# Transposes and value products of a segment loop, split into TensorE's four column groups

## The chip, the cores and the metric

The kernel runs on one core of one Trainium2 chip. The metric is the device time of one execution in microseconds (us). The engines are called as in the profile: PE is TensorE's matmul, PEld its weight load, DVE is VectorE, ACT is ScalarE, POOL is GpSimd, SP is SyncE, which only issues DMAs here.

## The reference

Two independent computations are put side by side in the output. Part A is attention with a recurrent memory: 64 segments of 32 rows, in each of which 8 memory rows and the segment's rows attend to each other, and the first 8 rows of the result are the next segment's memory. So the segments depend on each other in order. Part B is a long convolution with a state-space kernel; the change doesn't touch it.

```python
for s in range(n_seg):                       # 64 segments of 32 rows
    h = concatenate([mem, xs], axis=1)       # 8 + 32 rows of 1024
    q, k, v = (einsum('btd,dhe->bhte', h, W) for W in (Wq, Wk, Wv))   # 32 heads of 128
    scores = einsum('bhqe,bhke->bhqk', q, k) * scale
    p = softmax(where(mask, scores, -1e9))
    o = einsum('bhqk,bhke->bhqe', p, v)
    o = einsum('bhte,hed->btd', o, Wo)
    mem = o[:, :8]
    outs.append(o[:, 8:])
```

## The kernel before, in words

Part B and everything of part A that doesn't depend on the memory come first (some 700 us). Among the latter are q, k and v of the last 8 rows of every segment, which are kept in memory outside the core as PKd and VXd. The loop then runs over 64 segments with a state `hT` of 32 rows (24 rows of x, 8 of the memory), held as 8 chunks of 128 x 32. After the loop a last product (L617, some 55 us) finishes the output of the rows that were computed ahead.

A matmul has a stationary operand (loaded into the array by a weight load, PEld) and a moving one that streams through. The array's 128 output columns can be used as one, or as four column groups of 32, each with a weight load and a matmul of its own: `tile_position=(0, 32*g)`, with the output in partitions 32g to 32g+31. With 32 rows in `hT`, the large products of the loop use the groups:

- **Projections** (`quads`, L371): for each of 8 chunks (a unit, 128 x 2048 of a weight), four matmuls in the four groups, `hT` stationary, 512 columns of weight moving. The products are k0, q0, k1, q1, v0 and v1 (two halves of the heads).
- **Scores** (`scores`, L396 and L400): 32 matmuls in the groups, 40 columns moving.
- **Output projection** (`oproj`, L481): four matmuls in the groups for each head, 256 columns moving.

Between them stand pieces that use all 128 columns at once:

- **`tr`** (L382): four transposes of 128 x 128 turn the evacuated k or q (`evac`, L377) so that the head dimension lies on the partitions. They stand twice in a segment, eight at a time: k0 and q0 between the groups of k1, k1 and q1 between the groups of v0.
- **`pv`** (L450, L454): values times probabilities. V is stationary, and the spread-out probabilities `pb` (four matmuls) and those of the 8 ahead-computed keys, `lbs`, move. It is called four times in a segment: `pv_x` and `pv_l` for the first half of the heads, between the groups of v1; `pv_x` for the second half, inside the output projection; and `pv_l` for the second half, after it.
- **`tro`** (L580): two transposes of the new memory, which DVE copies into `hT` (L582). The next segment starts from there.

Around them, in the order written out by hand: ACT evacuates a projection (L377), copies a mask into the score buffer (L390), copies transposed q and k (L497, L517, L518; DVE L496 has k0), takes the exponentials (L416) and evacuates the products with the values (L467: `o0`, `o1`) and the result (L574). POOL adds the ahead-computed keys to KT (`put_kl`, L385, after the load of PKd) and spreads probabilities (L443, L438). DVE does the maxima, sums and 32 x 32 transposes of the softmax and spreads probabilities (L412 to L438: `pb`, `lb1`). L435 makes `pb`, and L438 makes `lb1`.

Most of the weights stay in the core. Twelve units of 512 KB in each segment don't fit and are streamed: SP issues them in order into four slots (`wst`, tags w0 to w3), and a slot is filled again when the matmuls that read it are done. Two units more are kept in PSUM and copied out by DVE (`fetch`, L292).

Of the kernel before, what the change touches and what calls it, by code (L numbers as in the profile page):

```python
# [30 lines left out]
        ("o", 15): (("Oa", 1024, 512), ("Ob", 1536, 384), (None, 1920, 128))}  # L31
HALF = (("q", 0, 7), ("o", 15))
SLOTS = 4

ARENA = 5984
AT = {"K7a": 3072, "K7b": 1024, "K7c": 2048, "K7d": 4192, "ob": 4960, "pk": 0, "vx": 3392, "Q7a": 2048, "Q7b": 3072,
# [21 lines left out]
def streamed_keys():  # L58
    return [key for key in [(m, t, kc) for (m, t), kcs in STREAM.items() for kc in kcs] + [("o", u) for u in STREAM_O]]
# [173 lines left out]
def part_a(ctx, tc, x, src, WD, HE, seg_len, out_a, ahead, W_res, rest, places, first):  # L233
    nc = tc.nc
# [13 lines left out]
    ident, mask, BD, BDx, BDL, hT = ahead.consts  # L248
# [6 lines left out]

    loads = [SLOTS]

# [36 lines left out]
    def stage(key, in_):  # L294
        t_ = wst.tile([128, 2048], BF16, name="wst", tag="w%d" % (loads[0] % SLOTS))
        loads[0] += 1
        nc.sync.dma_start(out=t_[:].rearrange("e (h d) -> e h d", h=2) if len(in_.shape) == 3 else t_[:], in_=in_)
        return t_

    def load_kept(key):  # L300
# [3 lines left out]
        if key in HALF:  # L304
            w = wst.tile([128, 2048], BF16, name="wst", tag="w%d" % (loads[0] % SLOTS))
            loads[0] += 1
# [56 lines left out]
    for s in range(NS):  # L363
        def quads(m, t, kcs, a=None):
            if a is None:
                a = ps.tile([128, 512], F32, name="acc", tag=BANK[m, t])
            for kc in kcs:
                w = unit((m, t, kc))
                for g in range(4):
                    for o_, rhs in columns(w, 512 * g, 512):  # L370
                        nc.tensor.matmul(a[32 * g:32 * g + 32, o_:o_ + rhs.shape[1]], lhsT=hT[:, kc, :], rhs=rhs,  # L371
                                         start=(kc == 0), stop=(kc == KC - 1), tile_position=(0, 32 * g), skip_group_check=True)
            return a
# [5 lines left out]

        def tr(q, p):  # L380
            for hl in range(4):
                nc.tensor.transpose(out=p[:, hl, :, :].rearrange("p a b -> p (a b)"), in_=q[:, 128 * hl:128 * hl + 128], identity=ident[:])  # L382

        def put_kl(KT, t):
            nc.gpsimd.tensor_copy(out=KT[:, :, :, SL:NK], in_=kl[t])  # L385
# [61 lines left out]

        def pv(p, t, V, pb, lbs):
            for hl in range(4):
                nc.tensor.matmul(p[:, hl, :], lhsT=V[:, 128 * hl:128 * hl + 128], rhs=pb[:, hl, :],  # L450
                                 start=(hl == 0), stop=False, skip_group_check=True)
            p, lo = p.rearrange("p a b -> p (a b)"), 0
            for lb in lbs:
                nc.tensor.matmul(p[:, lo:lo + lb.shape[1]], lhsT=vl[:, t, :], rhs=lb,  # L454
                                 start=False, stop=True, skip_group_check=True)
                lo += lb.shape[1]

        def pv_x(t, V, pb, lbs):

            p = ps.tile([128, 4, 128], F32, name="pv", tag="b1")  # L460
            pv(p[:], t, V, pb.rearrange("p a b c -> p a (b c)"), lbs)
            return p
# [7 lines left out]
        def pv_l(pl, t, V, L):  # L470

            pv(pl, t, V, L[:, 0].rearrange("p (a b) k -> p a (b k)", a=4), [L[:, 1].rearrange("p a k -> p (a k)")])
# [11 lines left out]
        a = quads("k", 0, (0, 2, 4, 6, 1, 3, 5, 7))  # L484
        k0 = evac(a, "k0")
        a = quads("q", 0, range(0, 6))
# [4 lines left out]
        a = quads("k", 1, range(0, 3))  # L491
        pq, pk_ = (ps.tile([128, 4, 4, SL], BF16, name="tr", tag=tag) for tag in ("b0", "b3"))
        tr(k0, pk_)
        tr(q0, pq)
        QT0, KT0 = at("QT0", 4, 4, SL), at("KT0", 4, 4, NK)
        nc.vector.tensor_copy(out=KT0[:, :, :, 0:SL], in_=pk_[:])  # L496
# [10 lines left out]
        a = quads("q", 1, range(KC))  # L507
# [3 lines left out]
        a = quads("v", 0, range(0, 3))  # L511
        p1 = ps.tile([128, 2, 4, 4, SL], BF16, name="tr", tag="b2")
        tr(k1, p1[:, 0])
        tr(q1, p1[:, 1])
        KT1, QT1 = at("KT1", 4, 4, NK), at("QT1", 4, 4, SL)
# [30 lines left out]
        a = quads("v", 1, range(0, 6))  # L546
        vl = vx[:, 0:256].rearrange("p (t e) -> p t e", t=2)
# [24 lines left out]
        osb = ob[:, 0, :]  # L572
# [4 lines left out]
        if s + 1 < NS:  # L577
            pt_o = [ps.tile([128, 4, SL], BF16, name="tro", tag=tag) for tag in ("b0", "b1")]
            for j in range(2):
                nc.tensor.transpose(out=pt_o[j][:].rearrange("p a b -> p (a b)"), in_=osb[:, 128 * j:128 * j + 128], identity=ident[:])  # L580
            for j in range(2):
                nc.vector.tensor_copy(out=hT[:, :, XM:SL].rearrange("p (q j) r -> p j q r", j=2)[:, j], in_=pt_o[j][:, :, XM:SL])  # L582
        if s + 1 < NS:
# [26 lines left out]
    for b in range(4):  # L610
        pe = [ps_k.tile([128, 512], F32, name="pe", tag="keep%d" % (2 * (b % 2) + n)) for n in range(2)]
        for u in order:
            for hh in range(2):
                h = 2 * u + hh
                hi = 16 * (h // 16) + 4 * (h % 4) + (h % 16) // 4
                for n in range(2):
                    nc.tensor.matmul(pe[n][:], lhsT=left[2 * b + hi // 16][:, 128 * (hi % 16):128 * (hi % 16) + 128],  # L617
                                     rhs=wo[u][:, 1024 * hh + 512 * n:1024 * hh + 512 * n + 512], start=(u == order[0] and hh == 0),
                                     stop=(u == order[-1] and hh == 1))
# [782 lines left out]
def kernel(  # L1402
# [34 lines left out]
    def residents(stay, early):  # L1437
# [26 lines left out]
        for _ in range(EARLY[1]):  # L1464
            load_resident(tc, pool, src, rest.pop(0), W_res)
            yield
        for i, key in enumerate([("k", 0, 7)] + streamed_keys()[0:SLOTS - 1]):
            first[key] = t_ = ahead.wst.tile([128, 2048], BF16, name="wst", tag="w%d" % i)
# [26 lines left out]
    with ExitStack() as ctx_a:  # L1495
        part_a(ctx_a, tc, A_x[0], src, WD, A_Wo.shape[0] * A_Wo.shape[1], seg_len, out_a, ahead, W_res, rest, places, first)
# [35 lines left out]
```

## Time and profile before

| | us |
|---|---|
| Time before, median of 3 runs | 2058.48 (2051.46 to 2060.06) |
| Span of the profiled execution, first to last instruction | 2054.6 |
| PE busy | 1873.8 (91%), 33734 matmuls |
| PEld busy | 1187.8 (58%) |
| DVE, ACT, POOL busy | 1413.7 (69%), 1051.7 (51%), 398.5 (19%) |
| L382, 1024 matmuls of 128 x 128 | 80.7 busy |
| L450, 512 matmuls of 128 x 128 into `pv` | 51.1 busy |
| L371, 12,288 matmuls and more on the loop's weights | the largest groups, 381 ns each from start to modelled end |

The profile gives no other time for the profiled execution than its span, which is 3.9 us under the median of the runs. Busy time of PE counts a matmul from its start to its modelled end, and matmuls overlap; what a piece of work takes is therefore read from the starts of neighbouring instructions in the timeline. A "segment" below is the time from one `tro` to the next.

### The profile page before, as it was taken

What the parts mean: (1) busy time and instruction counts of PE and PEld (TensorE: products, weight loads), DVE (VectorE), ACT (ScalarE), POOL (GpSimd) and SP (SyncE); (2) the same over time, 40 slices, a digit from 0 to 9 for tenths busy, and PEclk for the clock granted to TensorE, in tenths of its full rate; (3) what the DMA queues carried; (4) which work ended last, traced back from release to release, by engine and by line L of the source; (5) the groups of instructions that cost most, each with busy time, mean ns of one, the idle gap of its engine ahead of it and who ended that gap; (6) DMA issues with size and microseconds to landing.
All of it is one profiled execution on the core that took longest, in us unless ns stands there. A gap on an engine that the chain in (4) does not pass through costs nothing. (4 is left out here: it accounts for less than half of the span.)

```text
span 2054.6 us, 78607 instructions
## 1 busy us (share of the span) xinstructions
PE 1873.8 (91%) x33734; PEld 1187.8 (58%) x33734; DVE 1413.7 (69%) x3352; ACT 1051.7 (51%) x1981; POOL 398.5 (19%) x778
## 2 busy tenths in 40 slices
PE   2699999977999879999999999999999999999999
PEld 1365666666888535555555555555555555555554
DVE  8689989989999436666566666666666666656650
ACT  5899999961333324444344444444444444444430
POOL 2133343356000001111111111111111111111120
PEclk9999999989999989999999999999999999999999
DMA  7697986676646999999999999999999999999991
GB/s 192 176 247 217 262 227 181 164 207 204 217 140 190 330 328 350 349 337 335 315 347 342 343 339 342 343 342 339 347 345 333 339 332 341 335 333 339 342 356 46
DMA packets 349617, 590.25 MB, mean 287 GB/s; under 512 B 108536, under 2 KB 226520, under 8 KB 347220
## 3 DMA queue, kind: packets, MB, share of 16 engines
q1 hardware_dynamic: 294488, 526.49, 75.5%
q0 software_dynamic: 9968, 30.48, 4.5%
q10 hardware_dynamic: 44812, 28.26, 4.4%
q8 instruction: 264, 4.33, 0.9%
q14 instruction: 85, 0.70, 0.1%
HBM read 530.34 MB, written 65.26 MB: 290 GB/s over the span
## 5 line engine op out<-in xcount | busy, mean ns | idle before, releaser
L371 PEld LDWEIGHTS <-a_hT 128*32 128x32 bf16 x12352 | 334.4, 96 | 306.5 <-issue 59.4
L377 ACT CAST arena<-acc 128x512 bf16<-128x512 f32 x384 | 225.1, 586 | 375.6 <-PE acc L371 318.8
L371 PE MATMUL acc<-W,a_hT 128*32 128x512 bf16 x4608 | 371.7, 381 | 1.4 <-issue 1.2
L481 PEld LDWEIGHTS <-arena 128*32 128x32 bf16 x8256 | 212.1, 97 | 98.3 <-issue 47.1
L371 PE MATMUL acc<-wst,a_hT 128*32 128x512 bf16 x2304 | 231.9, 381 | 21.0 <-DMA wst<-WD_v 12.4
L292 DVE TENSOR_SCALAR arena<-keep 128x256 int32<-128x256 int32 (+1 forms) x512 | 176.3, 395 | 43.3 <-PE acc L371 39.8
L385 POOL COPY arena<-arena 128x128 bf16<-128x128 bf16 x128 | 37.5, 293 | 855.0 <-DMA arena<-PKd 312.3
L371 PE MATMUL acc<-MF,a_hT 128*32 128x512 bf16 x2048 | 171.3, 382 | 0.0
L481 PE MATMUL pp<-W_o,arena 128*32 128x256 bf16 x4096 | 138.4, 275 | 5.9 <-DMA W_o<-in_A_Wo_dram 5.8
L420 DVE TENSOR_REDUCE a_mx<-sc 128x4 f32<-128x160 f32 (+1 forms) x192 | 73.0, 380 | 81.8 <-ACT sc L416 81.8
L167 PE MATMUL pro<-xTl,wsl 128*128 128x512 bf16 x512 | 119.3, 384 | 9.6 <-ACT xTl L111 5.5
L412 DVE TENSOR_REDUCE a_mx<-sc 128x4 f32<-128x160 f32 (+1 forms) x192 | 72.0, 375 | 79.7 <-PE sc L400 78.2
L416 ACT ACTIVATE sc<-sc 128x160 f32<-128x160 f32 (+1 forms) x192 | 63.9, 333 | 120.9 <-DVE sc L413 101.8
L1066 PEld LDWEIGHTS <-MF 128*128 128x128 bf16 x1024 | 103.0, 101 | 29.9 <-issue 8.5
L443 POOL TENSOR_TENSOR arena<-arena,a_BD 128x128 bf16<-128x128 bf16 x128 | 71.2, 557 | 239.1 <-DVE arena L430 216.1
L496 DVE COPY arena<-tr 128x512 bf16<-128x512 bf16 x64 | 27.2, 425 | 128.3 <-PE tr L382 128.3
L1066 PE MATMUL hps<-KT,MF 128*128 128x256 bf16 x720 | 94.8, 285 | 14.0 <-DVE x L1235 11.0
L467 ACT CAST arena<-pv 128x256 bf16<-128x256 f32 (+1 forms) x192 | 79.0, 449 | 53.3 <-PE pp L450 41.0
L1293 PE MATMUL yp<-Bt,MI 128*128 128x256 bf16 x680 | 102.8, 273 | 0.8 <-ACT yb L1309 0.8
L574 ACT CAST arena<-pp 128x128 bf16<-128x128 f32 x128 | 27.7, 269 | 142.4 <-PE pp L481 142.4
L1104 ACT ACTIVATE E<-pa 128x648 bf16<-128x648 f32 x128 | 91.4, 714 | 17.6 <-PE pa L1096 12.1
L371 PE MATMUL acc<-W_v,a_hT 128*32 128x512 bf16 x1280 | 93.0, 380 | 0.5 <-issue 0.5
(314 smaller groups left out, 3988.2 us busy)
## 6 DMA issues: line engine op xcount, KB each, us to landing
wst<-WD_v SPq DMA_DIRECT2D x256, 512.0 KB
wst<-WD_k SPq DMA_DIRECT2D x192, 512.0 KB
wst<-WD_o SPq DMA_DIRECT2D x192, 512.0 KB
wst<-WD_q SPq DMA_DIRECT2D x128, 512.0 KB
Ud<-ux POOLq DMA_DIRECT2D x16, 1024.0 KB, 5.1
uq<-Ud SPq DMA_DIRECT2D x32, 512.0 KB
wsl<-in_A_Wk_dram SPq DMA_DIRECT2D x16, 512.0 KB
wsl<-in_A_Wv_dram SPq DMA_DIRECT2D x16, 512.0 KB
```

Of the source, the lines that this page charges most:

```text
L167: nc.tensor.matmul(a[:], lhsT=w[:, kc, 128 * j:128 * j + 128], rhs=xTl[:, kc, :, :].rearrange("p s k -> p (s k)"), start=(kc == 0), stop=( ...
L292: nc.vector.tensor_scalar(out=out.bitcast(I32), in0=in_.bitcast(I32), scalar1=0, scalar2=None, op0=ALU.bitwise_or)
L371: nc.tensor.matmul(a[32 * g:32 * g + 32, o_:o_ + rhs.shape[1]], lhsT=hT[:, kc, :], rhs=rhs, start=(kc == 0), stop=(kc == KC - 1), tile_pos ...
L377: nc.scalar.copy(out=q, in_=a[:])
L412: nc.vector.tensor_reduce(out=m_, in_=x, axis=AX.X, op=ALU.max)
L420: nc.vector.tensor_reduce(out=m_, in_=x, axis=AX.X, op=ALU.add)
L443: nc.gpsimd.tensor_tensor(out=L[:, 0].rearrange("p (a b) k -> p a b k", a=4), in0=bc(lt[:, :, 0:XL].unsqueeze(2), [128, 4, 4, XL]), in1=bc ...
L467: nc.scalar.copy(out=o[:, i:i + n], in_=p[:, i:i + n, :].rearrange("p a (g q) -> p a g q", g=4))
L481: nc.tensor.matmul(po[32 * qt:32 * qt + 32, o_:o_ + rhs.shape[1]], lhsT=oT[:, h % 4, (h % 16) // 4, :], rhs=rhs, start=False, stop=(h == 3 ...
L1066: pe.matmul(s_[r][half][:, cs, :], lhsT=MF[:, kc, 4 * rr + mc, cs, :], rhs=rhs, start=(i == 0 and mc == 0), stop=(i == 1 and mc == 3), ski ...
L1104: sc.activation(out=T["E", r, e // 4][:, lo:lo + 8 * NE].rearrange("p (i c) -> p i c", i=2), in_=T.pop(("p", r, e))[:, :, 0:4 * NE], func= ...
L1293: pe.matmul(yp[:, b, :], lhsT=m_[:, b, cs, kc, :], rhs=Bt[:, kc, j, half, c_, :], start=(kc == 0 and cs == 0 and half == 0), stop=(kc == 3 ...
```

## The change

The transposes in `tr` and `tro` and the products in `pv` are each written as four matmuls. Each takes 32 columns of the stationary operand, the whole moving operand as before, and writes 32 partitions of the same output through one column group. What is computed, the order of the pieces, and all work of other engines stay as they are. In every segment 39 matmuls with a 128-column stationary operand become 156 with 32 columns, and all matmuls of the loop then use the column groups.

```diff
+CT = (0, 32, 64, 96)
...
         def tr(q, p):
             for hl in range(4):
-                nc.tensor.transpose(out=p[:, hl, :, :].rearrange("p a b -> p (a b)"), in_=q[:, 128 * hl:128 * hl + 128], identity=ident[:])
+                for c in CT:
+                    nc.tensor.transpose(out=p[c:c + 32, hl, :, :].rearrange("p a b -> p (a b)"), in_=q[:, 128 * hl + c:128 * hl + c + 32],
+                                        identity=ident[:], tile_position=(0, c))
...
         def pv(p, t, V, pb, lbs):
             for hl in range(4):
-                nc.tensor.matmul(p[:, hl, :], lhsT=V[:, 128 * hl:128 * hl + 128], rhs=pb[:, hl, :],
-                                 start=(hl == 0), stop=False, skip_group_check=True)
+                for c in CT:
+                    nc.tensor.matmul(p[c:c + 32, hl, :], lhsT=V[:, 128 * hl + c:128 * hl + c + 32], rhs=pb[:, hl, :],
+                                     start=(hl == 0), stop=False, tile_position=(0, c), skip_group_check=True)
             p, lo = p.rearrange("p a b -> p (a b)"), 0
             for lb in lbs:
-                nc.tensor.matmul(p[:, lo:lo + lb.shape[1]], lhsT=vl[:, t, :], rhs=lb,
-                                 start=False, stop=True, skip_group_check=True)
+                for c in CT:
+                    nc.tensor.matmul(p[c:c + 32, lo:lo + lb.shape[1]], lhsT=vl[:, t, c:c + 32], rhs=lb,
+                                     start=False, stop=True, tile_position=(0, c), skip_group_check=True)
                 lo += lb.shape[1]
...
             for j in range(2):
-                nc.tensor.transpose(out=pt_o[j][:].rearrange("p a b -> p (a b)"), in_=osb[:, 128 * j:128 * j + 128], identity=ident[:])
+                for c in CT:
+                    nc.tensor.transpose(out=pt_o[j][c:c + 32].rearrange("p a b -> p (a b)"), in_=osb[:, 128 * j + c:128 * j + c + 32],
+                                        identity=ident[:], tile_position=(0, c))
```

## The prediction

> **What bounds the kernel now.** I read the page first for the share of each engine, then the table by stretch of time, then the waits, then the timelines of one segment on TensorE (PE), ScalarE (ACT) and VectorE (DVE). The change touches only the loop over 64 segments. From one `tro` to the next, the 61 segments between 745 and 1965 us take 19.0 us at the least, 19.6 in the median and 19.83 in the mean.
>
> ```profile
> 1000.00:1400.00 400.00, 385.71 (x8645) 226.16 (x8643) 253.22 (x797) 181.83 (x428) 58.99 (x142) 1.00 0.96 342
> ```
>
> Columns: stretch, its length, busy time of PE, weight loads, DVE, ACT and POOL, clock, DMA share, GB/s. In 400 us of the loop PE is busy for 386 at the full granted clock (1.00), and the DMA engines are busy for 0.96 at 342 GB/s. Two resources are nearly full at once, so time taken off PE isn't simply time won.
>
> ```profile
> 1229.60 0.41 PE L371 MATMUL acc<-wst,a_hT 128*32 128x512 bf16 x4
> 1229.93 0.62 PE L382 MATMUL tr<-a_ident,arena 128*128 128x128 bf16 x8
> 1230.48 0.40 PE L371 MATMUL acc<-W,a_hT 128*32 128x512 bf16 x4
> 1230.71 0.82 PE L371 MATMUL acc<-W_v,a_hT 128*32 128x512 bf16 x12
> 1231.36 0.39 PE L371 MATMUL acc<-wst,a_hT 128*32 128x512 bf16 x4
> 1231.77 0.28 PE L396 MATMUL sc<-arena 128*32 128x40 bf16 x16
> 1231.89 0.27 PE L400 MATMUL sc<-arena 128*8 128x40 bf16 x16
> 1231.99 0.63 PE L371 MATMUL acc<-W_v,a_hT 128*32 128x512 bf16 x8
> ```
>
> Columns are start, length, instruction, count; I use starts, since ends are modelled. A group of four L371 matmuls in the four column groups takes 0.216 us, start to start. Before the transposes, which are 128 columns wide (128*128), it takes 0.33: 0.115 more. The eight transposes follow each other every 0.056, 0.444 in all, yet the next L371 starts 0.55 after the first: 0.10 more (0.096 in the median). From L400 to L371, both in column groups, nothing is lost (0.10 for 16 matmuls that take 0.10). The same pair of losses stands at L450/L454.
>
> ```profile
> PEld L382 <- issue: 44.1, 110, 0.4
> POOL arena L385 <- DMA arena<-PKd: 312.3, 47, 7.7
> PEld L396 <- ACT arena L518: 30.3, 61, 0.5
> PEld L481 <- ACT arena L467: 41.5, 99, 0.8
> PE acc L371 <- DMA wst<-WD_v: 12.4, 19, 1.7
> PE pp L481 <- DMA wst<-WD_o: 9.8, 16, 1.1
> ```
>
> Waits: total us, times, longest. Before the transposes the weight load stands still for 0.4 us and waits for nothing that the profile shows; that is the loss above. The other lines are places where PE is early today and waits for something that PE doesn't speed up.
>
> **The change part by part.** *Count.* Per segment 16 transposes become 64, 2 become 8 (`tro`), and the 21 matmuls of `pv` become 84: 117 more matmuls, and as many weight loads. *Work in the groups:* I take it as unchanged. A round of four lasts as long as one matmul streams: 0.216 for 512 columns (L371), 0.109 for 256 (L481), 0.025 for 40 (L396: sixteen in 0.10 to 0.12). A round of 128 columns then lasts some 0.056, as one full transposition does. It is bounded by 0.053 below (half of L481's) and above by the fourth rival.
>
> *Switches.* Four stretches (first and second `tr`, first and second `pv`) each lose one 0.115 and one 0.096: 0.84 us a segment, 54 us in 64. That is all that could come off PE. The last `pv` and `tro` lie beside waits for ACT L574 and DVE L582, and gain nothing. What of the 0.84 reaches the end of the segment:
>
> - *First `tr` to the scores.* PE is 0.21 earlier at L396. It then needs the copy of QT, which ends 0.18 ahead of it today and moves with `tr` by up to 0.06, and POOL's L385, which waits for the DMA of PKd. In 27 of 61 segments L385 ends 0.05 before the scores, so it is what they wait for already: nothing is won there. Taking the least of the three in each segment, the mean is 0.09.
> - *Second `tr` in.* The chain goes on through ACT:
>
> ```profile
> 1230.65 0.59 ACT L517 COPY arena<-tr 128x512 bf16<-128x512 bf16 x1 [0.21 <-PE tr L382]
> 1231.13 0.59 ACT L518 COPY arena<-tr 128x512 bf16<-128x512 bf16 x1
> ```
>
>  ACT waits 0.21 for the transposes, so all of 0.115 moves the scores at 1231.77 (mean 0.11). *Second `tr` out:* nothing. The five groups of L371 after it take 1.288 instead of 1.08, because the scores wait for L518; the 0.096 only lengthens that wait.
> - *Both `pv`.* Behind the second scores the longest chain is DVE's:
>
> ```profile
> 1235.40 0.69 DVE L438 TENSOR_TENSOR arena<-arena,a_BDL 128x512 bf16<-128x512 bf16 x1
> 1236.00 0.32 DVE L412 TENSOR_REDUCE a_mx<-sc 128x4 f32<-128x160 f32 x1
> 1236.35 0.33 DVE L413 TENSOR_TENSOR sc<-sc,a_mx 128x160 f32<-128x160 f32 x1
> 1237.04 0.33 DVE L420 TENSOR_REDUCE a_mx<-sc 128x4 f32<-128x160 f32 x1 [0.35 <-ACT sc L416]
> ```
>
>  L438 makes `lb1`, ending 1236.09, and L454 reads it at 1236.20. L413 releases ACT's L416 and then L467 (`o1`), and in half of the segments L481 starts on `o1` 0.05 after that copy. An earlier `pv` waits at these two places. Only in segments that a weight transfer had held up is something left: 0.06 in the mean.
>
> Sum: 0.09 + 0.11 + 0.06 = 0.25 with rounding, times 64 = 16 us.
>
> *What the DMA takes back.* Twelve units of 512 KB a segment go through four slots, and a slot is refilled when its matmuls are done. From landing to first use a unit waits 0.42 us in the median, and 18% of the units wait under 0.1. One turn of the ring is a third of a segment, so each unit's margin shrinks by 0.25/3 = 0.084. The units with less margin than that lose 5 us over the loop (2 if it shrinks by 0.06, 23 by 0.2). Bounds: nothing, and all of the 16.
>
> *Instruction fetch.* 264 packets brought 78607 instructions; 64 × 234 = 15,000 more are some 50 packets. At 1 us each on one of 16 engines (0.9% of the span for 264) that is 3 us of DMA time, spread out: between 0 and 3 us. I take 0, since segments with four such packets are no longer than those with three.
>
> Sum: 2054.6 − 16 + 5 = 2043.6 us of span. The median of the runs is 2058.5, 3.9 above the span of the profiled run, so 2047.5.
>
> **The rivals.** *Transfers set the time.* With the DMA at 0.96, each stretch saved becomes a wait L371 <- wst: 2055 to 2060. For it: the units' margins. Against it: the fastest segments, 19.0 us, ran at up to 358 GB/s without a wait on `wst`.
>
> *The loss belongs to transposition, not to the switch of widths.* Then `tr` keeps it, and only the 0.06 behind `pv` is won, 4 us: 2055. Against it: L450/L454 transpose nothing and lose the same.
>
> *More of the 0.84 arrives.* If PKd lands earlier once the segments shorten and the DVE chain isn't what I take it for, the four ways in and two of the ways out count: 4 × 0.115 + 2 × 0.096 = 0.65, 42 us; less the DMA's share 2021.
>
> *Slower: small matmuls cost an issue slot each.* It decides once a matmul costs more than 0.014 us, a quarter of a 128-wide round. At 0.025 each, `tr` takes 32 × 0.025 = 0.80 against 0.66 with its losses, twice, and `tro` 0.2 against 0.11: 0.37 a segment, 24 us, 2082. If four groups didn't overlap at all, `tr` would take 1.78 and the loop lose over 150. Against it: L396 starts sixteen in 0.10, 0.006 each.
> The Trainium skill (TensorE: Matmul & The Clock Gate, "Wait — 56ns, not 53.3ns?") says that start-to-start never drops below about 25 ns. Taken per matmul it gives this rival's time; L396 shows 25 ns per round of four instead, so the trace bears it out only within one group.
> A second rule speaks against the change. TensorEngine Tiling ("Instruction Overhead") puts some 60 cycles on each matmul and warns against splitting what is already small. The transposes stream 128 columns, so by it the sum stays as it is; the 32-wide L450 gain nothing, and here they start every 0.025 already.
>
> **How the numbers follow.** Forecast, 2047.5, with its own range 2040 to 2052: 0.45. Transfers or transposition: 0.20. More arrives: 0.17. Slower: 0.18, with the issue slot at 0.12 and the added fetch traffic at 0.06 (a few us over 2058). A measurement of this kernel can tell about 0.5%, 10 us, so 2048 parts "faster" from "same" in the middle of the forecast. Two thirds of it (0.30) and all of "more arrives" are faster, 0.47; 0.15 and the second case are the same, 0.35; slower 0.18. The range goes from 2022, which leaves out the end of "more arrives", to 2070, which leaves out most of the issue slot.
>
> **What would show it.** Right: the L371 group before `tr` lasts 0.22 instead of 0.33, `tr` to the next L371 takes 0.45 instead of 0.55, "PEld L382 <- issue" is gone, the waits of L396 and of L481 on ACT grow, PE's wait on `wst` grows by some 5 us, and the DMA share rises towards 0.97. Wrong: `tr` longer than 0.55, starts of its matmuls more than 0.014 apart, or a loss still ahead of L382. I am wrong about the chain if the time falls by more than 20 us.

## The result, and the profile after

The changed kernel takes 2201.94 us in the median of 4 runs (2198.88 to 2204.5), against 2059.27 for the one before: ratio 1.0708, 95% interval 1.0678 to 1.0737. It is 143 us slower, 2.2 us a segment. Line numbers of the changed kernel are a little higher than before: L371 is now L372, L382 is L384, L396 and L400 are L399 and L403, L450 and L454 are L454 and L459, L481 is L486.

The same stretch of time as before, with the same columns (PE, weight loads, DVE, ACT, POOL busy, clock, DMA share, GB/s):

```profile
1000.00:1400.00 400.00, 338.22 (x9976) 215.74 (x9976) 231.57 (x723) 165.53 (x386) 53.34 (x130) 0.99 0.90 310
```

Both full resources have become less full: PE 338 us of 400 instead of 386, the DMA 0.90 at 310 GB/s instead of 0.96 at 342. Something else holds both up. First the timeline of PE around the second transposes, then a little later in the same segment:

```profile
1257.04 0.42 PE L372 MATMUL acc<-wst,a_hT 128*32 128x512 bf16 x4
1257.26 0.66 PE L384 MATMUL tr<-a_ident,arena 128*32 128x128 bf16 x32
1257.73 0.40 PE L372 MATMUL acc<-W,a_hT 128*32 128x512 bf16 x4
...
1260.65 0.42 PE L454 MATMUL pv<-arena 128*32 128x128 bf16 x16
1260.87 0.36 PE L459 MATMUL pv<-arena 128*32 128x384 bf16 x4
1262.52 0.24 PE L459 MATMUL pv<-a_S,arena 128*32 128x128 bf16 x4 [1.29 <-issue]
```

The upper part is what the change set out to do. The L372 group ahead of `tr` lasts 0.22 us instead of 0.33, the 32 small transposes take 0.47 until the next L372 instead of 0.55, and they start 0.014 apart. The lower part is new: in the middle of a `pv`, PE stands still for 1.29 us and waits for nothing that the profile knows ("issue"). The list of PE's waits shows how often:

```profile
PE pp L486 <- issue: 63.1, 54, 2.8
PE acc L372 <- issue: 39.7, 48, 2.1
...
PE pv L454 <- issue: 14.8, 13, 2.3
...
PE acc L372 <- DMA wst<-WD_v: 5.2, 8, 1.5
```

Summed over all lines from the loop to the end, "issue" is 181 us in 169 stops, where the kernel before had 5.3 us in 11. The stops are not tied to the lines that were changed: most stand at L486 and L372. What they share is their distance. Of 168 pairs of successive stops, 104 are 127 to 129 matmuls apart. Each matmul comes with one weight load, so that is 256 instructions. Counting matmuls and weight loads from the program's first, in the order of their starts, shows it without exception: all 169 stops stand before instruction 193 or 194 of a round of 256. The same two places hold all 11 stops of the kernel before and all 505 stops of the experiments below. The queue that brings instructions has the same unit; the first line is the kernel before, the second the changed one:

```profile
q8 instruction: 264, 4.33, 0.9%
q8 instruction: 323, 5.29, 1.0%
```

323 packets for 41216 matmuls and as many weight loads: one packet of 16 KB for 255 PE instructions, as before (33734 pairs, 264 packets).

An account of the 143 us: 176 more of "issue", 22 less of waiting for `wst` (26 before, 5 after, as PE now comes later than the weights), and 11 for the switches, of which more below: 176 − 22 − 11 = 143. That it closes so exactly is partly chance. It leaves out that in the loop PE ran for 51 us at half of the full clock (3 us before), in 14 spells, which is worth up to 26 us; and not every microsecond of idle time reaches the end.

### The profile page after: what moved, and what is told of

It is laid out like the page before. It is cut to its first block, busy times and chain, and to the rows that moved or that the text cites. A ratio compares the mean times of both kernels' runs of the same rounds, so it can differ in the third digit from the quotient of the medians.

```text
span 2197.2 us, 93570 instructions
## 1 busy us (share of the span) xinstructions
PE 1845.4 (84%) x41216; PEld 1227.6 (56%) x41216; DVE 1418.4 (65%) x3352; ACT 1055.1 (48%) x1981; POOL 399.5 (18%) x778
## 5 line engine op out<-in xcount | busy, mean ns | idle before, releaser
L372 PEld LDWEIGHTS <-a_hT 128*32 128x32 bf16 x12352 | 341.2, 97 | 333.5 <-issue 100.7
L378 ACT CAST arena<-acc 128x512 bf16<-128x512 f32 x384 | 225.1, 586 | 431.6 <-PE acc L372 363.6
L372 PE MATMUL acc<-W,a_hT 128*32 128x512 bf16 x4608 | 385.4, 383 | 18.4 <-issue 18.3
L486 PEld LDWEIGHTS <-arena 128*32 128x32 bf16 x8256 | 227.3, 98 | 145.5 <-issue 94.1
L372 PE MATMUL acc<-wst,a_hT 128*32 128x512 bf16 x2304 | 248.7, 385 | 13.2 <-issue 7.5
L486 PE MATMUL pp<-W_o,arena 128*32 128x256 bf16 x4096 | 151.0, 281 | 38.3 <-issue 32.9
L372 PE MATMUL acc<-MF,a_hT 128*32 128x512 bf16 x2048 | 175.9, 381 | 6.1 <-issue 6.1
L589 DVE COPY a_hT<-tro 128x32 bf16<-128x32 bf16 x126 | 20.6, 174 | 156.3 <-PE tro L586 156.2
L454 PEld LDWEIGHTS <-arena 128*32 128x32 bf16 x4096 | 84.6, 97 | 52.3 <-issue 38.7
L446 POOL TENSOR_TENSOR arena<-arena,a_BD 128x128 bf16<-128x128 bf16 x128 | 65.4, 511 | 227.6 <-DVE arena L433 159.7
```

Source lines behind the costliest of these rows:

```text
L378: nc.scalar.copy(out=q, in_=a[:])
L454: nc.tensor.matmul(p[c:c + 32, hl, :], lhsT=V[:, 128 * hl + c:128 * hl + c + 32], rhs=pb[:, hl, :], start=(hl == 0), stop=False, tile_posi ...
L486: nc.tensor.matmul(po[32 * qt:32 * qt + 32, o_:o_ + rhs.shape[1]], lhsT=oT[:, h % 4, (h % 16) // 4, :], rhs=rhs, start=False, stop=(h == 3 ...
```

## The experiments

The theory (A): PE's instructions arrive in blocks of 256, one block ahead at most, and a block takes some 5 us to become usable; the change made a segment need 4.2 blocks instead of 3.3, so a block lasts less than that. The rival (B): matmuls split by 32 columns are themselves slow somewhere.

**More instructions without a split into groups.** The output projection of the kernel before, cut in two by moving columns:

```diff
-                        for o_, rhs in columns(w, 1024 * hh + 256 * qt, 256):
+                        for o_, rhs in halved(u, columns(w, 1024 * hh + 256 * qt, 256)):
# halved (shortened here): for u < 15, each piece of 256 columns becomes two of 128
```

> The kernel before, with nothing split into column groups; instead 120 of the 128 output-projection matmuls of each segment (L481) are cut from 256 moving columns into two of 128 each, in the same group. That adds 240 instructions a segment (the change added 234) and no array time. Theory A (instruction fetch: PE's instructions come in blocks of 256, the next block is usable some 5.2 us after the last one, and a segment now needs 4.25 blocks instead of 3.3): PE idles without a stated wait at every 256th instruction, some 180 us in all, and as nothing is won from the switches the time is 2220 to 2245. Theory B (matmuls and transposes split by 32 columns are themselves slow, or the groups don't overlap): 2055 to 2070, as before.

Measured: 2285.06 us, ratio 1.1115 (1.1058 to 1.1172).

```profile
PE pp L484 <- issue: 173.1, 91, 4.8
```

"Issue" is 185 us, as expected, with nothing split by output columns: more instructions alone are enough, and B isn't needed. The time is 227 us above the kernel before, 40 over the upper end of what was expected. In the stretch from 1000 to 1400 us the granted clock is 0.94, where it was 1.00 before. The trace has it in spells: 38 times in the loop, mostly for 3.4 us, the granted clock is 0.5, 147 us in all, and each spell begins within 8 us after a pause of PE of more than 1.7 us. In a spell an L371 group takes 0.427 us instead of 0.216. That is worth up to 73 us, enough for the missing 40; it wasn't tried by itself.

**The same change with half of the weight traffic.** Two kernels, before and after, with this edit:

```diff
-        nc.sync.dma_start(out=t_[:].rearrange(...), in_=in_)
-        return t_
+        nc.sync.dma_start(out=t_[:, 0:1024], in_=in_[:, 0:1024])
+        return [(1024 * i, 1024, t_[:, 0:1024]) for i in range(2)]
```

> The changed kernel, but of each streamed weight unit only the first half is transferred (256 KB instead of 512) and read twice, so half of the streamed weights is left out. PE's instructions, the array time and all waits between engines stay. Theory A with the block's packet queued behind weight packets (it starts 2.7 us after the block before it became usable, and is usable 2.4 us after that): the queueing shrinks to 1 us or less, the next block needs 3.4 to 4 us, less than the 4.5 that a block lasts, the idle time without a stated wait falls from 179 us to under 20, and this kernel is 13 to 40 us FASTER than the kernel before with the same half stream. Theory A with a fetch time that doesn't depend on other transfers: still 100 us or more slower than that one. Theory B: some 140 us slower than that one.

> The kernel before, with the same half of the streamed weights left out: the partner of the run above. All theories: the waits for streamed weights (some 30 us) go, and the rest stays: 2010 to 2045.

Measured: 2001.47 with the change and 2000.93 without it. The 143 us are gone, and "issue" falls from 181 to 13 us; this is its largest line:

```profile
PE pp L486 <- issue: 3.8, 7, 0.9
```

So the blocks are late because of what else is being transferred, as A has it in its first form, and B is out: the same split matmuls cost nothing here. The kernel without the change came out 9 us below its expected range: nearly every segment takes 18.99 us, as the shortest did under the full stream. The hoped-for lead of 13 to 40 us isn't there either: the median segment is 0.17 us shorter with the change (18.82 against 18.99), 11 us over the loop, and the 13 us of "issue" that remain take that back.

**Parts and doses.** Four kernels add between 48 and 126 instructions a segment. First `tr` alone:

> Only the transposes of tr are split; the products with the values and the last two transposes stay 128 wide. Adds 96 instructions a segment, 3.7 blocks of 256. Theory A: a block lasts 5.3 us, near the 5.2 that the next one needs, so some blocks come late: 30 to 60 us of idle time, less some 12 us won from the switches: 2075 to 2110. Theory B: tr holds 48 of the 117 added matmuls and so some 58 of the 142 us: about 2117. If neither a split nor a fetch costs anything here: 2045.

Measured: 2101.35 (1.0174 to 1.0244 times before), "issue" 60 us. Then the same number of instructions without any switch taken away:

> The kernel before with 48 output-projection matmuls of each segment cut into two of 128 columns: 96 instructions added, as with the split tr alone, and no switch of widths taken away. Theory A: 60 us or more of idle time without a stated wait and nothing won: 2105 to 2135, some 11 us or more above the run with the split tr alone (2101). Theory B: 2058.

Measured: 2119.93 (ratio 1.0258 to 1.0331), "issue" 70 us. At equal count the kernel with the split transposes is 19 us faster (17 when each is compared with the kernel before of its own series): 10 for "issue", the rest is about what the switches are worth. Then the products with the values alone, and the first eight transposes alone:

> Only the products with the values (pv, four calls a segment) are split; all transposes stay 128 wide. Adds 126 instructions a segment (3.8 blocks of 256). Theory A (late instruction blocks), by the idle time without a stated wait found so far (5 us with 0 added, 60 with 96, 179 with 234, 185 with 240): some 80 to 90 us of it, and nothing won, since the chain behind the second scores is VectorE's: 2115 to 2140. Theory B (transposes in the groups are what costs): as before, 2058.

Measured: 2134.52 (1.0333 to 1.0387), "issue" 104 us. The time is as expected; the idle time is above the expected 80 to 90.

> Only the first eight transposes of a segment (k0 and q0) are split: 48 instructions added, and the two switches ahead of the first scores are gone, which the runs with half the streamed weights show to be worth 0.17 us a segment, 11 us in all. Theory A: a block of 256 lasts 5.6 us, 20 to 35 us of idle time, so 2065 to 2085, still no gain. If blocks come in time at this count: 2045 to 2050, faster than before.

Measured: 2069.52, ratio 1.0049 (1.0030 to 1.0067), "issue" 27 us. Even the part with the best return costs more than it brings.

| kernel | instructions added per segment | "issue", us | time, us |
|---|---|---|---|
| before | 0 | 5 | 2059 |
| 64-wide groups (below) | 32 | 14 | 2066 |
| first `tr` | 48 | 27 | 2070 |
| `tr` | 96 | 60 | 2101 |
| output projection cut, 48 | 96 | 70 | 2120 |
| `pv` | 126 | 104 | 2135 |
| the change | 234 | 181 | 2202 |
| output projection cut, 120 | 240 | 185 | 2285 |

The idle time follows the number of instructions, whichever line they are added to. The last row takes longer than its idle time accounts for, by the spells of half clock above.

**Many instructions in one place, at half the weight traffic.** The first experiment's cut on the light kernel:

> The kernel before with half of each streamed weight unit left out, and 120 output-projection matmuls a segment cut into two of 128 columns (240 instructions added). Theory A, with the block's packet queued behind weight packets: under 20 us of idle time and 2000 to 2025, where the same cut cost 227 us under the full stream. If cutting to 128 columns costs by itself, or a block's fetch is slow whatever else is transferred: 2150 or more.

Measured: 2103.51 us, with 87 us of "issue", most of it in the cut line:

```profile
PE pp L484 <- issue: 80.9, 66, 4.0
```

The expectation was wrong. It took blocks by the segment, as if the 4.25 of them were spread evenly. But the cut packs some 500 PE instructions into the output projection, about 3.5 us of array work, so a block lasts 1.75 us there. From 12 pairs of successive stops one block apart, a block takes 3.8 us in the median even at half the traffic. With only one block ahead, a dense stretch can't be covered by a sparse one before it. The packets show this too. In all traces together, each of the 685 stops ends some 2.4 us (2.2 to 2.9 for nine in ten) after the start of the latest packet. With packets and blocks numbered by that, from the loop on no packet starts more than 1.15 blocks before the place at which PE would stop for it.

**Groups of 64.** Whether the switch stands between groups and whole array, or between any two widths:

```diff
-                nc.tensor.transpose(out=p[:, hl, :, :]..., in_=q[:, 128 * hl:128 * hl + 128], identity=ident[:])
+                for c in (0, 64):
+                    nc.tensor.transpose(out=p[c:c + 64, hl, :, :]..., in_=q[:, 128 * hl + c:128 * hl + c + 64],
+                                        identity=ident[:], tile_position=(0, c))
```

> Both stretches of tr are split in two groups of 64 columns instead of four of 32: 32 instructions added a segment instead of 96. It tells whether the switch costs its 0.2 us between any two widths of group, or only between groups and the whole array. If any change of width is a switch: the group of L371 ahead of tr still lasts 0.31 us and the next one still starts 0.10 late, nothing is won, and the added instructions cost some 10 us of idle time: 2062 to 2072. If groups of 32 and of 64 go together: the two stretches are won as with four groups, some 11 us, against about 10 of late blocks: 2050 to 2062, no difference that counts.

```profile
1252.57 0.39 PE L371 MATMUL acc<-MF,a_hT 128*32 128x512 bf16 x4
1252.89 0.64 PE L383 MATMUL tr<-a_ident,arena 128*64 128x128 bf16 x16
1253.46 0.61 PE L371 MATMUL acc<-MF,a_hT 128*32 128x512 bf16 x8
```

Measured: 2065.84, ratio 1.0042 (1.0021 to 1.0063). The group ahead of `tr` still takes 0.32, and from the first transposition to the next L371 it is 0.57: a change between 32 and 64 is a switch too, and the cheaper split into 64 doesn't avoid it. The Trainium skill (TensorEngine Tiling, "Key Properties") states that a change of tiling mode drains the engine while another tile of the same mode doesn't; the trace agrees, and puts 0.115 us on the way in and 0.096 on the way out.

## Why the prediction was wrong, step by step

**The step that failed is "instruction fetch".** It counted the added packets nearly right (some 50; there were 59), though it divided all engines' 78607 instructions by 264 packets, where the packets of q8 fit PE's alone: 64 × 234 / 256 is 58.5. But it priced them as DMA work, 3 us spread over 16 engines, and took 0. The comparison on which it took 0, segments with four packets against segments with three, was made in a kernel whose blocks nearly always came in time, and couldn't show what a late one costs. What counts is when a block is there. In the changed kernel, from one stop to the next one block later, the block takes 5.1 us in the median (4.1 to 6.5 for nine in ten); these are the late blocks alone. Its packet starts 2.7 us after the block before it became usable, and PE goes on 2.4 us after the packet's start, of which the packet itself moves for 1. The first part is what the weight stream sets: in the light run with the cut it was 1.2 us, while the second, over all stops of that run, stayed at 2.4. Before the change a segment of 19.83 us used 3.3 blocks, 6.0 us each, and at 5.1 that left under a microsecond. With 4.2 blocks in an unhindered segment of some 19 us, a block lasts 4.5. So the margin lay in the profile: 264 packets and 33734 pairs give 256 instructions for each packet, and the packets' spacing gives the 6.0.

One rival did name the added fetch, with a chance of 0.06, but for a few us over 2058: the right place, and the same wrong price.

The Trainium skill (Runtime: NRT & Kernel Launch, "Instruction fetch mechanics") says that blocks of 256 instructions are brought while the one before runs and that crossing a boundary is mostly hidden. The unit agrees with the 255 measured here; "mostly hidden" held for the kernel before (5 us) and not for this one (181 us).

**The work in the groups**: right. A round of four 128-wide matmuls takes 0.056 (32 in 0.45 in the second `tr`). The rival "small matmuls cost an issue slot each" named the right sign for a wrong reason: starts are 0.014 apart in the mean, as in the forecast. "If four groups didn't overlap" came near in size (over 150 us) and is just as wrong.

**The switches**: right. All four ways in lost them, and so did the way out of the second `tr` and of the first `pv`. In the first `tr` half of the 0.096 on the way out now goes into a wait for q0's evacuation (ACT L378), and behind the second `pv` the wait for `lb1` hides it. The rival that put the loss on transposition falls with `pv`: the L371 group ahead of its first call took 0.35 before and takes 0.22 now.

**What reaches the end of the segment**: too high. The two light kernels show it without late weights. The first scores come 0.17 us earlier after the segment's first L371, in the median segment, and 0.14 earlier after `tro`, because the split `tro` takes 0.025 longer to the first L371 (0.521 against 0.496). The copy of QT sets this: it ended 0.18 ahead of the scores and now ends 0.05 ahead, and it comes 0.04 earlier itself. The 0.09 that I took allowed for PKd being late, and there the scores don't wait for it. For the second `tr` I took 0.11. The second scores do come another 0.10 earlier, but behind them only 0.03 is left:

```profile
1206.06 0.44 POOL L438 TENSOR_TENSOR arena<-arena,a_BDL 128x128 bf16<-128x128 bf16 x1
```

```profile
1206.40 0.43 DVE L435 TENSOR_TENSOR arena<-arena,a_BDx 128x512 bf16<-128x512 bf16 x1
1206.74 0.32 DVE L412 TENSOR_REDUCE a_mx<-sc 128x4 f32<-128x160 f32 x1
```

```profile
1204.08 0.44 POOL L441 TENSOR_TENSOR arena<-arena,a_BDL 128x128 bf16<-128x128 bf16 x1
```

```profile
1204.31 0.50 DVE L438 TENSOR_TENSOR arena<-arena,a_BDx 128x512 bf16<-128x512 bf16 x1
1204.73 0.31 DVE L415 TENSOR_REDUCE a_mx<-sc 128x4 f32<-128x160 f32 x1
```

The first pair is POOL and DVE of the light kernel before, the second pair the same two places with the change. DVE makes `pb` 0.34 us after the start of POOL's spreading before and 0.23 with the change, so more of it runs beside POOL: 0.22 us instead of 0.11 in the median segment. It takes 0.50 instead of 0.43, and DVE's next step gains 0.03 of the 0.10. That POOL is the reason wasn't tried by itself. Both `pv` gained nothing in the light runs; PE waits for `lb1` and `o1` instead, as the prediction had it. In all that is 0.14 + 0.03 = 0.17 a segment where 0.25 was forecast. DVE's chain carries it to the end: the last output-projection matmul reads weights that DVE copies out behind its softmax work (`a_S`, L292), and in the median segment it starts 0.05 after that copy in the kernel before and in both light kernels.

**What the DMA takes back**: not tested. PE's wait on `wst` fell from 26 to 5 us instead of growing, as PE was held up more than the weights. Nor did the DMA share rise; it fell to 0.90. So the rival "transfers set the time" isn't what happened either, though transfers are what makes the blocks late.

## What to carry to other kernels

Count the instructions of the densest engine, not only their time: divide them by 256 and compare how long a block lasts, in each stretch and not only in the mean, with how long the next one takes under the transfers that run beside it. A split into four that is free for the array multiplies the instructions by four, and an engine that streams weights beside a fully unrolled loop may have no room for them. "Idle <- issue" that turns up at lines nobody changed, at steps of 128 matmuls with their loads, is the sign, and so is one fixed place in every 256 instructions.

## What the runs showed of the hardware

- PE stopped for instructions only at one place in every round of 256 (number 193 or 194; 685 of 685 stops), and had at most one block ahead: no packet started more than 1.15 blocks before its place. With a block lasting 1.75 us in a dense stretch it stopped even when a block took only 3.8 us.
- A late block took 5.1 us in the median with the DMA engines moving some 305 GB/s (2.7 until its packet starts, 2.4 from there), and 3.8 at 174 GB/s.
- Matmuls in four groups start 0.014 us apart in the mean at 128 columns and 0.006 at 40, so a round of four costs what one matmul streams.
- A change between 128 or 64 columns and groups of 32 cost 0.11 to 0.12 us on the way in and 0.10 to 0.12 on the way out.
- After a pause of PE of more than 1.5 us the granted clock sometimes fell to half for 3.4 us or more: 38 spells in the run with the longest stops (4.8 us), 14 in the changed kernel, 1 before, none in the two light kernels without the cut.
- DVE's `pb` took 0.50 us with 0.22 us of POOL's spreading beside it, and 0.43 with 0.11 or none.
